# Turning both halves of a probability tile with one DMA in the first column group

## The chip, the cores and the metric

The kernel runs on one core of one Trainium2 chip. The core has a tensor engine (TensorE, PE, with its weight loads shown apart as PEld), a vector engine (VectorE, DVE), a scalar engine (ScalarE, ACT), a general engine (GpSimd, POOL), a queue engine (SyncE, SP) that issues DMAs, and 16 DMA engines. The metric is the device time of one execution in microseconds (us), less is better. Before the change it is 911.15 us, the median of three runs (909.12 to 911.76).

## The reference

The forward pass mixes two branches by a gate: `out = g * a + (1 - g) * b`, with `g = sigmoid(x . gate_w)`. Branch `a` is attention with 32 heads of 16 columns over 2048 rows, where row `q` sees the keys `q-255 ... q`; branch `b` is a gated feed-forward with 1376 hidden columns. The reference returns the output and, by automatic differentiation, the gradients of `x`, of the attention weights `wqkv` and `wo`, of the three feed-forward weights and of `gate_w`:

```
qkv = (x @ wqkv)                      # 32 heads of 16
scores = q k^T * 16**-0.5, masked to 0 <= q - k < 256
p = softmax(scores);  a = (p v) @ wo
b = ((relu(x Wg)) * (x Wu)) @ Wd
out, vjp = jax.vjp(f, x, wqkv, wo, Wg, Wu, Wd, gate_w);  grads = vjp(grad_out)
```

For the change only this matters: attention's backward pass needs the exponentials of the scores, P, and their products with the gradient scores, P*D, in both orientations. With keys on partitions they serve the sums over keys (output and gradient of q); turned, with queries on partitions, they serve the sums over queries (gradients of k and v).

## The kernel before

The program has three stages. The first (to about 258 us of the profiled span) does the feed-forward's forward and backward passes and writes three of its tensors to HBM. The second (258 to about 720 us) does attention, forward and backward, in four column groups `c` of 128 columns, that is 8 heads each. The third (to the end) forms the output and the gradient of `x` row block by row block.

The second stage is a list of turns (L633 to L661), 46 to a column group. A turn has two units (`x` = 0 and 1), each for two heads. A unit has one or two blocks of 128 queries by 128 keys. `pair_of(q)` is the diagonal block and the one below it for key block `q`; `edges_of` are the blocks at the window's far edge, two of them in one turn. For every two key blocks there are six turns, two of which are edge turns; every column group ends with four turns, the last with one block per unit.

In each turn the loop at L925 writes instructions in this order, by hand, and each engine runs its own in that order:
- `products` (L676): PE forms the scores S of this turn's two units and the gradient scores D of the turn before.
- `front` (L694): one exponential on ACT (L700) for both units, from S in PSUM to the tile `two` (called PP in the profile), 2 units x 2 kinds x 4 x 128 columns. Edge turns take the tile from another set, PPm. PP has 4 buffers and PPm 2.
- `mask` (L702): POOL zeroes what the window leaves out (L710).
- `gradp` (L714): one multiply on DVE (L717) writes P*D of the turn before, of both units, into the second half of the same tile.
- `flip` (L760) for units that are turned by DMA: one turn after their scores, on SP's queue.
- `some_sums`/`rowsum` (L726): PE multiplies P and P*D with K and V into the tile BA, at most five blocks a turn.
- `cd_piece` (L483): PE multiplies the turned tiles with the query rows into the tile CD (L492, L495), three turns or more after the query block is closed, in the order of key blocks.
- `flip` for the units that PE turns (L771): two turns after their scores, eight 128 x 128 transposes to PSUM, and a copy out (`share`, L80, which picks ACT or DVE by a running estimate; the copy is at L72 or L74).
- one or two pieces of background work: projections of the next rows and, from the second column group on, weight gradients.

So in the middle of the stage the unit `x` = 0 of every turn with two blocks is turned by a DMA of 8 blocks of 128 x 128 (256 KB), and the unit `x` = 1 by PE. Turns of the first two key blocks of the first column group, and of the last two of the last, are turned by PE alone. In the first column group there is no weight gradient yet in the background.

`place` (L743) gives a unit the tile of its turned blocks. For edge turns that is half of one of four `wide` tiles, taken once per turn; for others a tile of its own out of 14 (2 x 4 x 128 columns, 2 KB per partition each). The dictionary `P2` tells `cd_piece` where each block lies.

SP issues DMAs in the order written. In the stage these are the flips, the turned rows of Q and of the output's gradient (`rows`, L172, one per four row blocks), stores of finished rows (L506, 512 KB each), and loads of weights that the third stage needs (L523, turned on the way).

Of the kernel before, what the change touches and what calls it, by code (L numbers as in the profile page):

```python
# [11 lines left out]
BF = mybir.dt.bfloat16  # L12
# [10 lines left out]
def kernel(  # L23
# [20 lines left out]
    nc = tc.nc  # L44
    P = 128
# [9 lines left out]
    NT = S // P  # L55
    DC = D // P
# [23 lines left out]
    def share(out, in_, n, half=False, by=None, sbuf=False):  # L80
        cost = {"act": 0.11 + n * (0.00098 if sbuf else 0.00078),
                "dve": 0.08 + n * (0.00036 if sbuf else 0.00051 if half else 0.001)}
        eng = min(("act", "dve"), key=lambda e: busy[e] + cost[e])
        busy[eng] += cost[eng]
        if by is None:
            evac(out, in_, eng)
        elif eng == "act":
            nc.scalar.mul(out, in_, by)
        else:
            nc.vector.tensor_scalar(out, in_, by, None, op0=ALU.mult)  # L90
# [30 lines left out]
    def wide(name):  # L121
        return wq.tile([P, 2, 2, 4, P], BF, tag="m", bufs=4, name=name)
# [344 lines left out]
    if True:  # L467
# [4 lines left out]
        wk = p3b.enter_context(tc.tile_pool(name="attw", bufs=2))  # L472
# [3 lines left out]
        P2 = {}  # L476
# [157 lines left out]
        for c in range(DC):  # L634
            def pair_of(q):
                return [(q, q), (q + 1, q)]

            def edges_of(r):
                return [(k, k - 2) for k in (r, r + 1) if 2 <= k < NT]

            for q in range(0, NT, 2):
                if q + 2 < NT:
                    its = ((pair_of(q), 0), (pair_of(q), 2), (edges_of(q + 1), 0), (pair_of(q + 1), 2), (pair_of(q + 1), 0),
                           (edges_of(q + 2), 2))
                else:
                    its = ((pair_of(q), 0), (pair_of(q), 2), ([(q + 1, q + 1), (q + 1, q - 1)], 0), ([(q + 1, q + 1)], 2))
                for k, (blocks, g) in enumerate(its):
                    two = []
                    for x in range(2):
                        u = Unit()  # L650
                        u.c, u.q, u.g, u.x, u.blocks, u.nb, u.at = c, q + k // 3, g + x, x, blocks, len(blocks), len(turns_)
                        u.edge = blocks[-1][1] == blocks[-1][0] - 2
                        u.dma = x == 0 and len(blocks) == 2 and (c > 0 or q > 0) and (c < DC - 1 or q < NT - 2)
                        u.turn = u.at + (1 if u.dma else 2)
                        two.append(u)
                    turns_.append(two)
# [84 lines left out]
                BAsb[(u.c, qb)] = BAs  # L741

        def place(u):  # L743
            if u.edge:
                if u.at not in wides:
                    wides[u.at] = wide("p2")
                p2 = wides[u.at][:, u.x if u.nb == 2 else 0, :, :, :]
            elif u.nb == 2 or u.x == 0:
                p2 = wk.tile([P, 2, 4, P], BF, tag="P2", bufs=14, name="p2")[:]
                wides[u.at] = p2  # L750
            else:
                p2 = wides[u.at]
            for i, (qb, kb) in enumerate(u.blocks):
                b = 2 * (i if u.nb == 2 else u.x)
                P2[(u.c, qb, kb, u.g)] = p2[:, :, b:b + 2, :]
            return p2

        wides = {}

        def flip(u):  # L760
            p2 = place(u)
            if u.dma:
                nc.sync.dma_start_transpose(out=p2.rearrange("p a b q -> p (a b) q"),
                                            in_=u.PP.rearrange("p a b q -> p (a b) q"))
                return
            if u.nb == 2 or u.x == 0:
                pools["pt"] = ps.tile([P, 2, 4, P], BF, tag="tr", bufs=2, name="pt")
            pt = pools["pt"]
            for a in range(2):
                for b in range(2 * u.nb):  # L770
                    nc.tensor.transpose(pt[:, a, b if u.nb == 2 else 2 * u.x + b, :], u.PP[:, a, b, :], ident[:])  # L771
            return (lambda: share(p2, pt[:], 8 * P, True)) if u.nb == 2 or u.x == 1 else None
# [102 lines left out]
        with tc.manual_schedule():  # L875
# [49 lines left out]
            while turn < NI + 3 or ev or cdq or bg or sums:  # L925
# [9 lines left out]
                if us and (turn == 0 or turns_[turn - 1][0].q != us[0].q):  # L935
                    c, j = us[0].c, us[0].q
# [32 lines left out]
                for v in vs:  # L969
                    if v.dma:  # L970
                        flip(v)
# [10 lines left out]
                for w in flips.get(turn, []):  # L982
                    if not w.dma:
                        for f in copies:
                            f()
                        copies = [f for f in [flip(w)] if f]
# [165 lines left out]
```

## Time and profile before

| | |
|---|---|
| median of three runs | 911.15 us |
| the profiled execution's own time | 905.92 us |
| its span on the core | 904.2 us |
| mean granted TensorE clock | 0.992 |
| PE busy | 865.2 us, 96% |
| DVE, POOL, ACT busy | 492.8, 474.5, 389.9 us |
| transposes on PE (L771) | 1536, 117.9 us busy |
| copies of turned tiles on DVE (L74) | 167, 684 ns each |
| DMAs that turn tiles (L763) | 168, 4.4 us from issue to landing (median) |
| SP's DMA queue q1 | 133.13 MB, 81.7% of 16 engines' time |

Busy time of an engine is the time that its instructions cover; PE's matmuls overlap each other, so one of them may be listed with 220 ns and come 50 to 60 ns after the last. The share of a DMA queue is the time that its packets took, as a part of 16 engines' time; a packet that waits for its turn counts too, so a share near 100% does not say by itself that bytes move at the highest rate. "To landing" is the time from an issue to the last byte's arrival.

The first column group's turns lie between 258.04 us (its first exponential) and 360.96 us (the first of the second group).

### The profile page before, as it was taken

To read this page: it belongs to the slowest core of one execution; us is meant where nothing else is said; L and a number is where in the kernel's file an instruction comes from. 1 tells how busy PE (TensorE), PEld (TensorE's weight loads), DVE (VectorE), ACT (ScalarE), POOL (GpSimd) and SP (SyncE) were. 2 spreads that over 40 slices of the span, in tenths; PEclk is the share of its full clock that TensorE was granted. 3 is DMA by queue.
4 is the path that set the end of the run, shared out by engine and by line. 5 is a ranking of instruction groups with operands and counts; after the bars stand their busy time and mean duration, and the time that the engine had idled before them with its cause. 6 is when DMAs were issued, how large, how long until landed. Compare 5 with 4: busy or idle time off the path is not lost. (4 is left out here: it accounts for less than half of the span.)

```text
span 904.2 us, 29627 instructions
## 1 busy us (share of the span) xinstructions
PE 865.2 (96%) x12569; PEld 563.4 (62%) x12569; DVE 492.8 (55%) x754; ACT 389.9 (43%) x565; POOL 474.5 (52%) x883
## 2 busy tenths in 40 slices
PE   7999999999988999999999999999899999999998
PEld 4566555565657777777777767777577744444443
DVE  4543322233247888878778777788677322322322
ACT  5522222223247676666557655667464311111111
POOL 2544444454327777976668766687566512222221
PEclk9999999999989999999999999999899999999999
DMA  9989899988726999999978999999999996777750
GB/s 282 210 182 228 214 209 201 225 202 199 191 56 96 149 148 170 146 152 217 181 113 140 132 238 161 135 164 173 219 178 216 248 278 155 187 196 193 195 124 27
DMA packets 444334, 161.25 MB, mean 178 GB/s; under 512 B 362696, under 2 KB 441896, under 8 KB 444200
## 3 DMA queue, kind: packets, MB, share of 16 engines
q1 hardware_dynamic: 418520, 133.13, 81.7%
q10 hardware_dynamic: 23856, 20.98, 8.2%
q0 software_dynamic: 1824, 5.25, 1.7%
q8 instruction: 98, 1.61, 0.7%
q14 instruction: 36, 0.29, 0.1%
HBM read 38.44 MB, written 38.41 MB: 85 GB/s over the span
## 5 line engine op out<-in xcount | busy, mean ns | idle before, releaser
L717 DVE TENSOR_TENSOR PP<-PP,D 128x1024 bf16<-128x1024 bf16 (+1 forms) x184 | 219.5, 1193 | 69.4 <-POOL PP L710 24.9
L700 ACT ACTIVATE PP<-S 128x1024 bf16<-128x1024 f32 (+1 forms) x184 | 185.2, 1006 | 96.3 <-PE D L667 48.2
L710 POOL TENSOR_SCALAR_AFFINE_SELECT PP<-PP 128x512 bf16<-128x512 bf16 (+1 forms) x188 | 143.5, 764 | 108.8 <-ACT PP L700 93.4
L74 DVE COPY p<-pt 128x1024 bf16<-128x1024 bf16 x167 | 114.3, 684 | 16.5 <-PE pt L771 16.3
L771 PE MATMUL pt<-ident,PP 128*128 128x128 bf16 x1536 | 117.9, 221 | 1.7 <-DVE p L74 0.9
L350 POOL TENSOR_TENSOR hT<-rg,upm 128x512 bf16<-128x512 bf16 x44 | 52.4, 1192 | 126.1 <-DVE upm L348 105.4
L734 PE MATMUL BA<-KV,PP 128*128 128x33 bf16 x1440 | 106.6, 180 | 6.1 <-ACT BAs L72 6.1
L383 PE MATMUL wps<-dgu_r,x_r 128*128 128x256 bf16 x704 | 105.6, 272 | 3.7 <-DVE wst L74 3.4
L734 PEld LDWEIGHTS <-PP 128*128 128x128 bf16 x1440 | 85.6, 96 | 31.2 <-issue 11.2
L736 PE MATMUL BA<-KV,PP 128*128 128x17 bf16 x1440 | 102.2, 170 | 0.3 <-issue 0.3
L492 PE MATMUL CD<-rq,p 128*128 128x32 bf16 x1440 | 95.0, 176 | 0.0
L495 PE MATMUL CD<-rq,p 128*128 128x16 bf16 x1440 | 93.8, 169 | 1.1 <-issue 1.1
L736 PEld LDWEIGHTS <-PP 128*128 128x128 bf16 x1440 | 84.7, 96 | 13.5 <-issue 8.6
L383 PEld LDWEIGHTS <-x_r 128*128 128x128 bf16 x704 | 68.8, 98 | 35.7 <-issue 5.4
L771 PEld LDWEIGHTS <-PP 128*128 128x128 bf16 x1536 | 89.5, 98 | 2.0 <-issue 2.0
L667 PE MATMUL S<-zT,K 32*128 32x128 bf16 (+3 forms) x1056 | 78.4, 241 | 5.4 <-ACT PP L700 2.7
L495 PEld LDWEIGHTS <-p 128*128 128x128 bf16 x1440 | 80.6, 96 | 1.5 <-issue 1.2
L492 PEld LDWEIGHTS <-p 128*128 128x128 bf16 x1440 | 80.8, 96 | 0.3
L667 PE MATMUL D<-zT,V 32*128 32x128 bf16 (+3 forms) x1056 | 73.3, 239 | 4.1 <-DVE PP L717 3.6
L1072 ACT COPY a_sb<-aps 128x512 f32<-128x512 f32 x16 | 9.4, 586 | 145.9 <-issue 133.0
L348 DVE SCALAR_TENSOR_TENSOR upm<-rg,ups 128x512 bf16<-128x512 bf16 x44 | 30.2, 686 | 68.5 <-PE ups L336 43.8
L385 PE MATMUL dps<-db_r,h_r 128*128 128x512 bf16 x176 | 66.7, 379 | 0.0
(144 smaller groups left out, 1471.4 us busy)
## 6 DMA issues: line engine op xcount, KB each, us to landing
dqkvo_d<-rows_st SPq DMA_DIRECT2D x14, 512.0 KB, 4.7
hT_d<-hT ACTq DMA_DIRECT2D x44, 128.0 KB, 2.5
dgT_d<-dgu ACTq DMA_DIRECT2D x44, 128.0 KB, 2.9
duT_d<-dgu ACTq DMA_DIRECT2D x44, 128.0 KB, 2.8
duT_g<-duT_d SPq DMA_DIRECT2D x8, 640.0 KB, 5.3
dgT_g<-dgT_d SPq DMA_DIRECT2D x7, 640.0 KB, 8.0
gt<-hT_d SPq DMA_DIRECT2D x7, 640.0 KB, 5.8
dar<-da_d SPq DMA_DIRECT2D x16, 256.0 KB, 4.6
```

What stands on the lines that cost most here:

```text
L74: nc.vector.tensor_copy(out, in_)
L383: nc.tensor.matmul(acc["w"][:, c, :], lhsT=x_r[:, t, c * P:(c + 1) * P], rhs=k.dgu_r[:, :, i, :], start=(go_ and c % 2 == 0), stop=no_, sk ...
L385: nc.tensor.matmul(acc["d"][:], lhsT=k.h_r[:, i, :], rhs=db_r[:, t, :], start=go_, stop=no_)
L492: nc.tensor.matmul(cd[0][:, h, :], lhsT=p2[:, 0, pr, :], rhs=rq[:, h, 0:2 * Dh], start=cd[1], stop=True, skip_group_check=True)
L495: nc.tensor.matmul(cd[0][:, h, 0:Dh], lhsT=p2[:, 1, pr, :], rhs=rq[:, h, 2 * Dh:3 * Dh], start=False, stop=True, skip_group_check=True)
L667: nc.tensor.matmul(dst, lhsT=proj[(u.c, kb // TPG)][nm + ("", "1")[par]][rows[par], (kb % TPG) * P:(kb % TPG + 1) * P], rhs=proj[(u.c, qb ...
L700: nc.scalar.activation(two[:].rearrange("p x a b q -> p x a (b q)")[:, :, 0, 0:n], flat(us[0].S[:], n), ACT.Exp)
L710: nc.gpsimd.affine_select(out=out, in_=out, compare_op=ALU.is_ge, fill=0.0, base=0 if up else -1, pattern=[[0, 2], [0, b1 - b0], [1 if up ...
L717: nc.vector.tensor_tensor(out=v(1), in0=v(0), in1=flat(vs[0].D[:], n), op=ALU.mult)
L734: nc.tensor.matmul(BA[:, h, 0:33], lhsT=u.PP[:, 0, 2 * i + pr, :], rhs=kv[:, kb % TPG, h, 1:34], start=(first and pr == 0), stop=True, ski ...
L736: nc.tensor.matmul(BA[:, h, 33:50], lhsT=u.PP[:, 1, 2 * i + pr, :], rhs=kv[:, kb % TPG, h, 0:17], start=False, stop=True, skip_group_check ...
L771: nc.tensor.transpose(pt[:, a, b if u.nb == 2 else 2 * u.x + b, :], u.PP[:, a, b, :], ident[:])
```

## The change

In the first column group, from the third key block on, a turn with two blocks per unit has both units turned by one DMA of 16 blocks (512 KB). It is issued when the second unit's turn to flip comes, which for both is one turn after the scores. These units are turned on PE no longer, so their transposes and the copies out of PSUM are gone: 39 turns, 312 transposes, 39 copies. The number of SP's DMAs stays at 39 there.

For all column groups, the turned tiles of a turn that is not an edge turn lie in one tile of double size, 7 of them in place of 14 single ones. The bytes are the same. In the other column groups the first unit is still turned by DMA and the second by PE.

```diff
                         u.edge = blocks[-1][1] == blocks[-1][0] - 2
-                        u.dma = x == 0 and len(blocks) == 2 and (c > 0 or q > 0) and (c < DC - 1 or q < NT - 2)
+                        u.joint = c == 0 and q > 0 and len(blocks) == 2
+                        u.dma = (x == 0 or u.joint) and len(blocks) == 2 and (c > 0 or q > 0) and (c < DC - 1 or q < NT - 2)
                         u.turn = u.at + (1 if u.dma else 2)
...
         def place(u):
-            if u.edge:
-                if u.at not in wides:
-                    wides[u.at] = wide("p2")
-                p2 = wides[u.at][:, u.x if u.nb == 2 else 0, :, :, :]
-            elif u.nb == 2 or u.x == 0:
-                p2 = wk.tile([P, 2, 4, P], BF, tag="P2", bufs=14, name="p2")[:]
-                wides[u.at] = p2
-            else:
-                p2 = wides[u.at]
+            if u.at not in wides:
+                wides[u.at] = wide("p2") if u.edge else wk.tile([P, 2, 2, 4, P], BF, tag="P2", bufs=7, name="p2")
+            p2 = wides[u.at][:, u.x if u.nb == 2 else 0, :, :, :]
...
         def flip(u):
             p2 = place(u)
+            if u.joint:
+                if u.x == 1:
+                    nc.sync.dma_start_transpose(out=wides[u.at][:].rearrange("p x a b q -> p (x a b) q"),
+                                                in_=u.two[:].rearrange("p x a b q -> p (x a b q)"))
+                return
             if u.dma:
                 nc.sync.dma_start_transpose(out=p2.rearrange("p a b q -> p (a b) q"),
                                             in_=u.PP.rearrange("p a b q -> p (a b) q"))
```

## The prediction

> **What bounds the kernel now.** I read the page first (busy shares, then the DMA line), then the attention stage by its first column group alone: its groups of lines, its DMA traffic, and windows of one to two microseconds in it. The change touches only that group. Its exponentials (L700) count the turns: the first turn starts at 258.04 us, turn 6, the first that has a joint DMA, at 272.27, and the next column group starts at 360.96.
>
> The page's parts 1 and 3:
>
> ```profile
> PE 865.2 (96%) x12569; PEld 563.4 (62%) x12569; DVE 492.8 (55%) x754; ACT 389.9 (43%) x565; POOL 474.5 (52%) x883
> ...
> q8 instruction: 98, 1.61, 0.7%
> ```
>
> TensorE (PE) is busy everywhere, so 39 x 8 transposes less on it look like time won. Keep queue q8 in mind: 98 packets for 2 x 12569 PE and PEld instructions, one per 256 of them. These are fetches of PE's program.
>
> The DMA view of 277 to 359 us (the stage of the change; GB/s in 40 slices, packets, queues, issues):
>
> ```profile
> GB/s 52 79 128 73 189 191 138 160 165 131 128 71 168 95 113 153 114 277 194 88 268 109 192 136 128 136 128 128 72 226 238 70 194 270 96 264 96 226 146 166
> DMA packets 45179, 12.30 MB, mean 150 GB/s; under 512 B 44135, under 2 KB 45159, under 8 KB 45159
> q1 hardware_dynamic: 45159, 12.01, 100.8%
> q8 instruction: 15, 0.25, 1.2%
> dqkvo_d<-rows_st SPq DMA_DIRECT2D x2, 512.0 KB, 4.6
> p<-PP SPq DMA_TRANSPOSE x38, 4.2
> rows<-zT SPq DMA_TRANSPOSE x3, 4.9
> p<-in_A_wqkv_dram SPq DMA_TRANSPOSE x2, 3.9
> ```
>
> SP's queue already shows a share of 100.8% at 150 GB/s, while the slices swing between 70 and 277. A share near 100% can be time in which packets wait, so the next view asks what the queue can do. It is the windows view (PE, PEld, DVE, ACT and POOL busy; PE clock; DMA share; GB/s):
>
> ```profile
> 277.00:359.00 82.00, 79.11 (x1973) 62.32 (x1970) 72.12 (x103) 58.98 (x76) 64.95 (x146) 1.00 1.02 150
> 340.90:357.30 16.40, 16.18 (x405) 12.45 (x404) 14.33 (x21) 11.02 (x16) 12.85 (x31) 1.00 1.26 165
> 740.80:743.80 3.00, 3.00 (x16) 1.37 (x14) 0.40 (x1) 0.11 (x1) 0.58 (x1) 1.00 1.27 290
> 317.90:319.30 1.40, 1.09 (x32) 0.89 (x30) 1.25 (x2) 0.91 (x2) 0.78 (x1) 1.00 1.26 281
> 316.50:317.90 1.40, 1.40 (x36) 0.96 (x35) 1.26 (x2) 0.96 (x2) 1.35 (x4) 1.00 0.18 6
> 278.50:279.80 1.30, 1.30 (x28) 0.78 (x19) 1.30 (x2) 1.10 (x2) 0.79 (x4) 1.00 1.06 199
> ```
>
> Three rates of the same transposing traffic are to be seen. With a full queue it runs at 281 to 290 GB/s (740.8 is the 32-block transpose of L872). With an empty queue it runs at 199. And for 1.4 us, from 316.5, it stands at 6: in the packet records a q8 fetch of 16 KB starts at 316.02 and holds one of the 16 engines for 1.09 us, and the other engines' transposing packets stop until that engine has caught up. The packets of the stage show such a stop of 1.3 to 1.6 us beside almost every fetch. Where SP issues transposes without a pause (340.9 to 357.3, three fetches), 165 GB/s is what comes out.
>
> **The change part by part.** The turn now: 39 turns from 272.27 to 358.94, 2.22 us each.
>
> *PE transposes.* 39 units of 8 leave PE. One unit, from the timeline:
>
> ```profile
> 296.31 0.46 PEld L771 LDWEIGHTS <-PP 128*128 128x128 bf16 x8
> ```
>
> 39 x 0.45 us = 17.6 us of PE, all on PE's own path: 79.11 of 82 us are busy. This is the most that the change can win. POOL with 64.95 of the 82 us bounds it at about the same place (17 us).
>
> *Copies.* 39 copies of the transposed tiles leave: 33 of DVE at 684 ns (L74) and 6 of ACT at 1012 ns (L72). That is 22.6 and 6.1 us beside PE's work. DVE has 72.12 of 82 us in this stage, so this makes room and sets no end.
>
> *The wait of the DMA.* The joint DMA needs both halves of the tile PP. One multiply (L717) writes both, so it waits for nothing that the old DMA did not wait for, and it stands at the same place in SP's queue. The second half is now turned a turn earlier. Its first reader on PE (L492) comes 6 to 10 turns after its scores, in the order of the built program.
>
> *The tile of a turn.* 7 tiles of double size in place of 14: both halves of a turn are read by the same steps of L492, so the rotation frees them at the same turns as before. Nothing.
>
> *DMA work.* This is the price. 39 DMAs move 512 KB in place of 256 KB. 38 more x 262 KB are 10 MB on top of the 12.30: 22.3 MB where the queue has moved 12.3. Per turn, as S:
> - 524 KB at the rate of a full queue, 290 GB/s: 1.81 us.
> - Fetches: 15 now, 13 after, since 39 x 16 PE and PEld instructions less are 624 / 256 = 2.4 of them. 13 x 1.4 us / 39 turns = 0.47 us.
> - What else shares the queue: 3 + 2 transposes of 262 KB and 2 stores of 524 KB, 2.36 MB at 290 GB/s, 8.1 us, 0.21 us per turn.
> Sum 2.49 us, more than the turn's 2.22.
>
> The lower end is S = 2.02, no stop at all: a fetch that hits an engine while the others work on. The upper end is the rate of 340.9 to 357.3, 165 GB/s with its stops inside: 3.18 + 0.37 = 3.55. I take 2.60, near the sum, because a queue that is behind is a full one, and full queues show 281 to 290; the tenth is for stretches in which it runs dry. SP's time to issue 16 blocks is in no row: 8 blocks take 1.23 us at least, 32 take 5.9 and more (L872), while SP waits for room. Within S that lies between 1.3 and 2.9 us, and only the upper end would bind.
>
> The Trainium skill (Advanced Engine Details and Errata, X-Bar Transpose) says that transposing DMAs are as fast as plain ones and expects 350 to 400 GB/s. At 350 the 22.3 MB would take 64 us and would hide in the 82. This trace speaks against it: no window of transposes is above 290, and the stage's mean is 150 at a full share.
>
> *How late DMAs become time.* The tiles PP have 4 buffers for two turns in three and PPm 2 for the third, so the exponential of a turn waits until the DMA of the turn six before has read its tile. Now a DMA lands 4.4 us after issue (median) and nothing waits. With S above the turn, the queue falls behind until this wait binds, and then ACT, POOL, DVE and PE all go at S. The first joint DMA is issued at 277.32 and lands 4.4 + 0.9 us later, at 282.6. The DMA of turn 43 lands 37 x S later. It frees the tile of turn 49, whose exponential now starts at 367.02. The loss is 282.6 + 37 S - 367.02 = 37 S - 84.4 us: none at S = 2.28, 7.7 at 2.49, 11.8 at 2.60. After that the next column group turns 8 blocks by DMA per 2.46 us and the queue catches up; it is full of PE's work, so nothing is given back.
>
> PE's clock: it would idle some 25% of the stage. In 270 to 275 us it was busy 3.33 of 5 us and kept its full clock, so I count nothing; the half clock from 259.2 to 266.0 came after longer gaps and would cost some 3 us each time.
>
> Against the profiled execution: 905.92 + 11.8 = 917.7 us. Its span is 904.2, and the 1.7 around it stay. The median of the runs shown is 911.15, 5.2 above that execution, and the change is added to it: 911.15 + 11.8 = 923.
>
> **Rivals.**
> A, the faster side: fetches do not stop the joint transposes. For it: some fetches in the stage fall where the queue was empty and cost nothing. Against it: the six GB/s at 316.5 and the slices of 70 to 96. Then S = 2.02, 37 S - 84.4 = -9.7 us, 901. It decides from S below 2.28, where the stops cost less than 0.26 us per turn. The skill's rate above ends on this side too: then PE's 17 us would be all won, 894.
>
> B, the queue is fed no faster than an empty one runs: 199 GB/s (278.5 to 279.8), because SP issues late and each DMA starts from nothing. Then (524 + 60) KB / 199 = 2.93 us, plus a third of the stops that the feed doesn't cover, 3.1: +30 us, 941. For it: 165 GB/s in the stretch without pauses, where SP's issues follow each other at 1.4 us. Against it: 281 after each stop, in this same stage.
>
> C, nothing to be measured: S between 2.21 and 2.35. A change of 0.3% (2.7 us) is about what a measurement can tell from none.
>
> **How the numbers follow.** The forecast, S from 2.35 to 2.85: 0.50. B and beyond: 0.18. A: 0.20, of which 0.03 for the skill's rate. C: 0.12. So slower 0.68, same 0.12, faster 0.20. The time is that of S = 2.60, 923. The forecast's own range is 914 to 932. The 8 in 10 leave out a tenth of A's side and about a tenth of B's: 903 to 942.
>
> **What would show it.** In the profile after: the stage from 272 to 361 us longer, its GB/s near 220 and no slices of 70 to 130 but those of the fetches; DMAs p<-PP of the stage that land 9 to 13 us after issue; SP's issue of them over 2 us; ACT's exponentials waiting for "DMA p<-PP"; PE busy about 70% there. The page's chain would have to gain nothing after 740 us. Right in the sum, wrong in S: landings of 5 us and turns near 2 us. Wrong altogether: landings that stay below 6 us with turns still above 2.2, so that something other than the DMA holds the turn, or a half PE clock in the stage.

## The result and the profile after

The changed kernel takes 942.41 us, the median of four runs (939.37 to 945.54), against 911.39 us for the kernel before (four runs, 909.12 to 911.76). The ratio is 1.0348, with a 95% interval of 1.0315 to 1.0381: 31 us slower. The forecast was slower by 11.8 us, 923 us, its own range was 914 to 932, and its eight in ten ended at 942.

The profiled execution took 942.83 us, with a span of 941.1 us. Parts 1 and 2 of its page:

```profile
PE 856.1 (91%) x12130; PEld 553.9 (59%) x12257; DVE 475.0 (50%) x720; ACT 384.5 (41%) x560; POOL 474.7 (50%) x883
...
PEclk8999999999997655689999998999999999999999
...
GB/s 274 199 178 216 206 210 212 221 202 199 172 18 185 201 186 204 188 174 179 191 160 108 162 179 162 167 150 157 209 187 210 221 272 234 176 171 177 202 140 29
```

PE is busy for 9 us less, and yet the span is 37 us longer. TensorE's clock is low for long in one place, slices 13 to 18 (282 to 424 us), which is the first column group from its first joint DMA on, and the start of the second. By the first exponential of each column group, the first group takes 129.7 us (262.19 to 391.93) where it took 102.9, and the second 118.4 where it took 114.1. Together that is 31 us. Another 4 us of this execution lie ahead of attention, in work that the change does not touch, and 2 us in the third column group; after that both kernels take 314 us to the end.

The windows view of the stage (PE, PEld, DVE, ACT and POOL busy; PE clock; DMA share; GB/s):

```profile
281.00:391.00 110.00, 76.17 (x1699) 51.74 (x1713) 57.09 (x74) 54.83 (x72) 67.54 (x151) 0.65 1.18 192
```

No engine is busy for 70% of it. The DMA view of the same window, and what the line of the joint DMA says (its durations on SP in ns, who waited for it, issue to landing), with the line of the 8-block DMAs in the kernel before ahead of it:

```profile
q1 hardware_dynamic: 79557, 20.82, 117.2%
q8 instruction: 13, 0.21, 0.7%
```

```profile
L763 SPq DMA_TRANSPOSE p<-PP x168: 1231/1297/4285, 277.3 to 703.1; - x168
...
L759 SPq DMA_TRANSPOSE p<-PP x39: 1397/2591/4376, 281.1 to 399.2; - x39
...
  ACT PP L701: 41.4, 17
...
DMA to landing us min/median/max: 4.4/5.4/7.2
```

ACT's exponentials wait 17 times, 41.4 us in all, for a joint DMA; in the kernel before, nothing waited for one of the DMAs that turn tiles (L763). SP is occupied by one joint DMA for 2.6 us (median), where the 8-block ones took 1.3. The stretch from the timeline of SP, and that of ACT:

```profile
332.96 19.52 SPq L759 DMA_TRANSPOSE p<-PP  x7
```

```profile
346.93 1.02 ACT L701 ACTIVATE PP<-S 128x1024 bf16<-128x1024 f32 x1 [1.33 <-DMA p<-PP]
348.65 1.02 ACT L701 ACTIVATE PP<-S 128x1024 bf16<-128x1024 f32 x1 [0.70 <-PE D L668]
...
353.11 1.02 ACT L701 ACTIVATE PP<-S 128x1024 bf16<-128x1024 f32 x1 [2.26 <-DMA p<-PP]
...
398.56 1.02 ACT L701 ACTIVATE PP<-S 128x1024 bf16<-128x1024 f32 x1 [5.61 <-DMA p<-PP]
...
402.50 1.02 ACT L701 ACTIVATE PP<-S 128x1024 bf16<-128x1024 f32 x1 [1.09 <-PE S L668]
```

In this stretch SP issues one joint DMA behind the other without a pause, one per 2.8 us. Turn by turn the records show the wait of six turns: the multiply of turn 24 ended at 325.10, its DMA was issued at 336.12, when SP was through with those ahead of it; it landed at 340.58, and the exponential of turn 30, which writes the same tile, started at 340.69. Of the 29 exponentials of turns 18 to 46, 23 start within 0.15 us of the landing six turns back. The joint DMAs land 3.12 us apart on the mean (285.62 to 404.22, 38 intervals).

### The profile page after: what moved, and what is told of

Read it like the earlier page. It is cut to its first block, busy times and chain, and to the rows that moved or that the text cites. A ratio compares the mean times of both kernels' runs of the same rounds, so it can differ in the third digit from the quotient of the medians.

```text
span 941.1 us, 28831 instructions
## 1 busy us (share of the span) xinstructions
PE 856.1 (91%) x12130; PEld 553.9 (59%) x12257; DVE 475.0 (50%) x720; ACT 384.5 (41%) x560; POOL 474.7 (50%) x883
## 5 line engine op out<-in xcount | busy, mean ns | idle before, releaser
L711 POOL TENSOR_SCALAR_AFFINE_SELECT PP<-PP 128x512 bf16<-128x512 bf16 (+1 forms) x188 | 143.3, 763 | 142.2 <-ACT PP L701 127.0
L735 PEld LDWEIGHTS <-PP 128*128 128x128 bf16 x1440 | 87.7, 98 | 36.8 <-issue 18.9
L668 PE MATMUL S<-zT,K 32*128 32x128 bf16 (+3 forms) x1056 | 83.1, 256 | 26.0 <-ACT PP L701 21.8
L737 PEld LDWEIGHTS <-PP 128*128 128x128 bf16 x1440 | 86.3, 98 | 31.1 <-issue 27.9
L74 DVE COPY p<-pt 128x1024 bf16<-128x1024 bf16 x134 | 91.8, 685 | 15.5 <-PE pt L771 15.2
L771 PE MATMUL pt<-ident,PP 128*128 128x128 bf16 x1224 | 94.8, 223 | 1.0 <-DVE p L74 0.9
L495 PEld LDWEIGHTS <-p 128*128 128x128 bf16 x1440 | 81.6, 97 | 1.8 <-issue 1.5
L668 PE MATMUL D<-zT,V 32*128 32x128 bf16 (+3 forms) x1056 | 79.2, 255 | 3.5 <-DVE PP L718 2.7
L492 PEld LDWEIGHTS <-p 128*128 128x128 bf16 x1440 | 81.9, 97 | 0.3
L668 PEld LDWEIGHTS <-K 16*128 16x128 bf16 (+1 forms) x1056 | 36.7, 97 | 68.5 <-issue 61.9
L771 PEld LDWEIGHTS <-PP 128*128 128x128 bf16 x1224 | 72.3, 99 | 1.2 <-issue 1.2
```

The source lines that it names most:

```text
L74: nc.vector.tensor_copy(out, in_)
L492: nc.tensor.matmul(cd[0][:, h, :], lhsT=p2[:, 0, pr, :], rhs=rq[:, h, 0:2 * Dh], start=cd[1], stop=True, skip_group_check=True)
L495: nc.tensor.matmul(cd[0][:, h, 0:Dh], lhsT=p2[:, 1, pr, :], rhs=rq[:, h, 2 * Dh:3 * Dh], start=False, stop=True, skip_group_check=True)
L668: nc.tensor.matmul(dst, lhsT=proj[(u.c, kb // TPG)][nm + ("", "1")[par]][rows[par], (kb % TPG) * P:(kb % TPG + 1) * P], rhs=proj[(u.c, qb ...
L711: nc.gpsimd.affine_select(out=out, in_=out, compare_op=ALU.is_ge, fill=0.0, base=0 if up else -1, pattern=[[0, 2], [0, b1 - b0], [1 if up ...
L735: nc.tensor.matmul(BA[:, h, 0:33], lhsT=u.PP[:, 0, 2 * i + pr, :], rhs=kv[:, kb % TPG, h, 1:34], start=(first and pr == 0), stop=True, ski ...
```

## The experiments

One theory was tried against four rivals. The theory: SP's DMA queue needs more time for a turn's bytes than the turn had, and the loss is 37 S - 84.4 us, with S the queue's time per turn. The rivals: the form of one DMA with 16 blocks; the tile of double size; PE's half clock; a turn that would not have been faster with PE relieved. The chips differ, so each kernel has its ratio to the kernel before on the same chip, whose medians were 909.4 to 911.5 us.

**The tile alone.**

```diff
-                        u.joint = c == 0 and q > 0 and len(blocks) == 2
+                        u.joint = False
```

> Only the second part of the change: turned tiles of a turn in one tile of double size, 7 in place of 14; no joint DMA. Theory (DMA queue: the joint DMAs' bytes set the turn): as before, 911 within 3 us. Rival (the tile's rotation makes DMAs wait): some part of the 31 us, above 915.

Measured: 911.23 us, ratio 0.9995 [0.9971, 1.0019]. The tile of double size costs nothing that can be seen; the interval is -2.6 to +1.7 us.

**Two DMAs of 8 blocks in place of one of 16.**

```diff
             if u.joint:
-                if u.x == 1:
-                    nc.sync.dma_start_transpose(out=wides[u.at][:].rearrange("p x a b q -> p (x a b) q"),
-                                                in_=u.two[:].rearrange("p x a b q -> p (x a b q)"))
+                nc.sync.dma_start_transpose(out=p2.rearrange("p a b q -> p (a b) q"),
+                                            in_=u.PP.rearrange("p a b q -> p (a b) q"))
                 return
```

> Both units of a turn are turned by DMA, but each by its own DMA of 8 blocks, both issued one turn after the scores. Same bytes as the changed kernel. Theory (bytes in SP's queue set the turn): 937 to 948, turns of 3.0 to 3.2 us in the first column group. Rival (a DMA of 16 blocks is a slow form, its issue or its flow): below 925.

Measured: 949.74 us, ratio 1.0422 [1.0395, 1.0450], 7 us slower than the changed kernel and a little outside the range. The form of 16 blocks is not the trouble; for these bytes it is the better form. The last experiment comes back to this.

**PE's transposes kept.** The joint DMA stays, and PE turns the second unit as well, into PSUM, for nobody.

```diff
+                for w in (turns_[turn - 2] if 2 <= turn <= NI + 1 else []):
+                    if w.joint and w.x == 1:
+                        idle_turn(w)       # 8 transposes into a PSUM tile "tr"
```

> The changed kernel, and PE still does the eight transposes of the second unit into PSUM, two turns after the scores; nobody reads them and the copies stay out. PE has 17.6 us more to do and less time to idle. Theory (DMA queue): 939 to 946, with a granted clock nearer 1. Rival (PE's half clock, which the idle time brings, makes the loss): below 925.

Measured: 943.62 us, ratio 1.0343 [1.0312, 1.0373]. With PE's work put back the time is that of the changed kernel. The windows view of its stage:

```profile
281.00:390.00 109.00, 86.77 (x2003) 67.24 (x2003) 55.07 (x72) 52.23 (x70) 66.06 (x146) 0.86 1.18 191
```

The clock is 0.86 in place of 0.65, PE has 312 transposes more to do, and the queue moves its bytes at the same pace, 191 GB/s against 192. So PE's work is not in this time, and its clock, as far as 0.86 against 0.65 can tell, is not either.

**The second unit not turned.** The DMA of 8 blocks stays, and nothing turns the second unit.

```diff
-                if u.x == 1:
+                if u.x == 0:   # 8 blocks, of the first unit
...
-            p2 = wides[u.at][:, u.x if u.nb == 2 else 0, :, :, :]
+            p2 = wides[u.at][:, u.x if u.nb == 2 and not u.joint else 0, :, :, :]
```

> The first unit is turned by a DMA of 8 blocks as before the change, the second unit is not turned at all: its products read the first unit's turned blocks. Left out: the second unit's turned blocks in the first column group. It has the change's relief of PE, DVE and ACT without its DMA bytes. Theory (DMA queue): faster than before, 895 to 906, since PE's 17.6 us are partly won and the queue needs about 2.0 us per turn. Rival (a PE with less to do clocks down and the turn's chain of engines is the bound anyway): 908 or more.

Measured: 909.01 us, ratio 0.9972 [0.9957, 0.9987], 2.5 us faster than before. So even with its price left out, the relief of PE by 17.6 us, DVE by 22.6 and ACT by 6.1 brings 2.5 us. The theory's range, 895 to 906, was missed, and the rival's, 908 or more, was met. The windows show one thing that this rival names, a lower clock:

```profile
290.00:308.00 18.00, 15.85 (x416) 11.33 (x413) 12.52 (x18) 12.69 (x18) 15.09 (x34) 0.97 0.98 141
308.00:325.00 17.00, 16.32 (x342) 10.66 (x338) 10.13 (x13) 10.22 (x13) 12.53 (x28) 0.50 1.18 170
325.00:352.00 27.00, 24.23 (x621) 17.19 (x620) 19.75 (x27) 19.25 (x27) 23.50 (x53) 1.00 1.08 156
```

From 308 to 325 us TensorE had half its clock and did 342 matmuls in 17 us (20 per us); in the windows beside it, at 0.97 and 1.00, it did 23 per us. It had idled 12% of the first window; at half clock its records cover 96% of the second.

**The same, with a little work for PE.** Added to the last kernel: four transposes per turn that nobody reads, in place of the eight that the kernel before did.

```diff
+            for b in range(2 * u.nb):
+                nc.tensor.transpose(pt[:, 0, b, :], u.PP[:, 0, b, :], ident[:])
```

> The kernel in which the second unit is not turned (its products read the first unit's turned blocks; that part is left out), and PE does four transposes per turn whose result nobody reads, in place of the eight of before. It asks why that kernel won only 2.5 us of PE's 17.6: its clock fell to half for some 25 us of the stage. If the clock ate the gain: clock near 1 in the stage, turns of 2.0 to 2.1 us, 903 to 907. If the turn's chain of ACT, DVE and POOL is the bound anyway: 909 or more, turns near 2.2.

Measured: 904.61 us, ratio 0.9942 [0.9920, 0.9964], 5.3 us faster than before. By the two ratios, more work on PE made it 2.7 us faster; the interval of each ratio is 1.4 to 2 us to either side. The windows view of the same stretch:

```profile
308.00:325.00 17.00, 15.32 (x415) 12.27 (x418) 11.70 (x16) 11.31 (x15) 14.63 (x31) 1.00 1.15 178
```

Here the clock held. From 277 to 358 us it was 0.96 on the mean, where the kernel without the four transposes had 0.85 (277 to 357). The two profiled executions don't show the gain, though: 907.01 and 906.86 us, with turns of 2.17 us in both, where turns of 2.0 to 2.1 had been expected. Among the ten executions of this kernel time and clock go together: the six with a mean clock of 0.988 or more took 901.99 to 905.38 us, the four at 0.987 or less 906.58 to 909.61. That the clock took those 2.7 us is therefore likely and not shown.

In the Trainium skill, "TensorE: Matmul & The Clock Gate" (Part 1, What's actually happening) says that the gate passes half the clock after an idle window of about 3.4 us. Its two states are the ones seen here, 0.5 and 1.0, and the stretch of 17.07 us at half clock is five times its window of 3.41 us. The page speaks of idle windows; here the clock fell with PE's matmuls covering 88% of the window before (83% of its last 3.41 us), in many short waits.

**The dose.** The joint DMA in one turn in six, one in three, two in three; each kernel has one of the three new lines.

```diff
-                        u.joint = c == 0 and q > 0 and len(blocks) == 2
+                        u.joint = c == 0 and q > 0 and len(blocks) == 2 and k == 2          # 7 of 39 turns
+                        u.joint = c == 0 and q > 0 and len(blocks) == 2 and u.edge          # 13 of 39
+                        u.joint = c == 0 and q > 0 and len(blocks) == 2 and not u.edge      # 26 of 39
```

> The joint DMA in one turn in six of the first column group (the first edge turn of each six and the edge turn at the end, 7 joint DMAs). Theory (queue), 16 blocks in 2.5 us and 0.6 us of stops and other DMAs: 9.4 blocks on the mean, S = 1.46 + 0.6 = 2.06 us, below the turn's 2.22 and the 2.28 from which a loss begins. PE is relieved of 7 x 0.45 = 3.2 us, of which some 60% were won where nothing else was in the way: 908 to 911, against a kernel before at 910 to 911.5. Rival (any joint DMA hurts): above 912.

> The joint DMA in the edge turns alone, one turn in three (13 joint DMAs of 16 blocks; the other 26 turns as before the change). Theory (queue), with the changed kernel's own figures, 16 blocks in 2.5 us, 0.37 us of fetch stops and 0.25 us of other DMAs per turn: 10.7 blocks on the mean, S = 1.67 + 0.62 = 2.29 us, and the loss 37 S - 84.4 = 0.3 us: 909 to 915. Rival (each joint DMA costs in proportion, by a wait of its own): a third of 31 us, 921.

> The joint DMA in all but the edge turns, two turns in three (26 joint DMAs). Theory (queue): 13.3 blocks on the mean, S = 2.08 + 0.62 = 2.70 us, loss 37 x 2.70 - 84.4 = 15.5 us: 923 to 931. Rival (in proportion): two thirds of 31 us, 932.

| joint turns | S by the theory, us | loss by 37 S - 84.4, us | measured, us | ratio (95%) |
|---|---|---|---|---|
| 7 | 2.06 | none | 909.04 | 1.0003 [0.9982, 1.0025] |
| 13 | 2.29 | 0.3 | 912.39 | 1.0035 [1.0011, 1.0059] |
| 26 | 2.70 | 15.5 | 925.24 | 1.0161 [1.0128, 1.0193] |
| 39 | 3.12 (measured) | 31.0 | 942.41 | 1.0348 [1.0315, 1.0381] |

The loss is not in proportion: by the medians, the first 13 joint DMAs cost 2.4 us, the next 13 another 12.9, the last 13 another 15.7. So there is a threshold, between 7 and 26 joint turns, and the theory has it near 13. None of these kernels is faster than the one before. The seven joint DMAs were expected to win about 2 us by PE's relief; nothing of it is to be seen, and the interval ends at -1.6 us. That 15.5 and the 15.3 us of the medians agree so closely at 26 is partly luck: in the profiled execution the DMAs landed 2.78 us apart (turns 6 to 43) and not 2.70, the formula makes 18.5 us of that, and its first two column groups took 19.4 us longer than those of the profiled execution before.

**The rate by itself.** A program without the computation: transposes of 16 blocks from SBUF to SBUF on SP's queue, in stretches, each beside one kind of the attention stage's work. It was executed once.

```diff
+    for other in (None, lambda: dve(26), lambda: pl(40), lambda: act(30), lambda: pe(560), all4):
+        tc.strict_bb_all_engine_barrier()
+        turn16(12)
+        if other is not None:
+            other()
+    tc.strict_bb_all_engine_barrier()
+    turn8(24)
```

> Not the reference's computation: a program that only measures the disputed rate, with all outputs zero. Seven stretches, each of 12 transposes of 16 blocks from SBUF to SBUF on SP's queue (the last of 24 of 8 blocks): alone, beside DVE multiplies as L717's, beside POOL selects as L710's, beside ACT exponentials as L700's, beside PE matmuls with weight loads as L734's, beside all four, and last the 8-block ones alone. If 2.5 us per 16 blocks (210 GB/s) is the queue's own pace for transposes within SBUF, all stretches show 200 to 215 GB/s. If it comes from the engines' traffic in the attention stage, the first shows 280 to 290 (1.81 us) and one of the others falls to 210.

The windows view, in the order of the stretches (alone; DVE; POOL; ACT; PE; the stretch meant for all four; 8 blocks alone), then PE's stretch before its first fetch, and that fetch. In the sixth stretch ACT's work came only after its DMAs, from 207.7 us on, so DVE, POOL and PE are beside them there:

```profile
12.00:40.00 28.00, 0.00 (x0) 0.00 (x0) 0.00 (x0) 0.00 (x0) 0.00 (x0) 1.00 1.13 210
44.00:72.00 28.00, 0.00 (x0) 0.00 (x0) 27.25 (x23) 0.00 (x0) 0.00 (x0) 1.00 1.13 210
77.00:105.00 28.00, 0.00 (x0) 0.00 (x0) 0.00 (x0) 0.00 (x0) 22.85 (x36) 1.00 1.14 211
109.00:137.00 28.00, 0.00 (x0) 0.00 (x0) 0.00 (x0) 27.14 (x28) 0.00 (x0) 1.00 1.13 210
142.00:173.00 31.00, 12.58 (x464) 12.25 (x461) 0.00 (x0) 0.00 (x0) 0.00 (x0) 0.70 1.15 187
178.00:206.00 28.00, 12.11 (x459) 11.68 (x455) 27.25 (x23) 0.00 (x0) 22.84 (x36) 0.80 1.22 195
242.00:272.00 30.00, 0.00 (x0) 0.00 (x0) 0.00 (x0) 0.00 (x0) 0.00 (x0) 0.50 1.01 191
140.50:143.30 2.80, 2.80 (x106) 2.80 (x103) 0.00 (x0) 0.00 (x0) 0.00 (x0) 1.00 1.16 206
143.40:145.00 1.60, 1.60 (x67) 1.60 (x64) 0.00 (x0) 0.00 (x0) 0.00 (x0) 1.00 1.25 30
```

Alone, with a full queue, 16 blocks run at 210 GB/s, 2.50 us. DVE, POOL and ACT, each by itself beside them, change nothing (210, 211, 210). Beside PE it is 187, and in that stretch lie four fetches of its program: at 143.4 the rate falls to 30 GB/s. From 140.5 to 143.3, where PE works and no fetch has come yet, it is 206 GB/s, so the loss comes with the fetches and not with PE's work. 187 GB/s over 31 us are 5.8 MB, which at 210 take 27.6, so the four fetches cost 3.4 us, 0.85 each. In the sixth stretch the same count gives 2.0 us for three to four fetches, 0.5 to 0.7 each; in the changed kernel's window, 20.82 MB in 110 us, it leaves 10.9 us for 13 fetches, 0.84 each. They cost less than they last because the queue catches up after each: in the records some 1120 packets per us for about 2 us, 287 GB/s, where it otherwise moves 835. The stretch with 8 blocks runs at 191 GB/s with one issue per 1.375 us, 2.75 us for 16 blocks: 0.25 more per turn, 10 us over 39 turns, where two DMAs in place of one had cost 7. SP is occupied for 1.33 us by each of these issues and they land 3.2 to 3.5 us after it, so nothing piles up behind them: this pace may be SP's own and not the queue's, which was not tried.

## Why the prediction was wrong

The step that failed is a term of the sum: "524 KB at the rate of a full queue, 290 GB/s: 1.81 us". It is 2.50 us. The two windows that carried it were something else. The one at 317.9 us is a queue that catches up after a fetch, which in the changed kernel's records lasts 1.1 to 2.9 us and no longer. The one at 740.8 us is a transpose whose source lies in HBM; in the records it too follows half a microsecond of near standstill, so which of the two made it fast is not known. The third window, 199 GB/s, was read as a queue that starts from nothing; it was near the pace itself. With the measured figures the sum comes near: 2.50 for 16 blocks, 14 fetches x 0.85 / 39 = 0.31, and 2.36 MB of other DMAs, by an estimate at 210 GB/s too, 11.2 us / 39 = 0.29, give S = 3.10; with 0.5 us a fetch it is 2.97. Measured: 3.12. The forecast's S was 2.60.

What the other steps made of it, one by one:
- The loss as a function of S was right: 37 x 3.12 - 84.4 = 31.0 us, and 31.0 us were measured. As S is taken from the same run, this tests the formula alone, and the agreement to the tenth is luck. The last wait for a joint DMA is that of turn 47, at 398.56, whose tile turn 42's DMA frees; turn 49, from which the formula was made, started at 402.50 after a wait for PE, 2.5 us after its tile came free. From turn 47, which started at 363.38 before, the formula would be 282.6 + 36 S - 363.38, 31.5 us at 3.12. The threshold of 2.28 us agrees with the dose.
- Rival B had the price, S = 3.1 and 941 us, and a chance of 0.18. Its mechanism was half right: not, with 16 blocks, that SP issues late, but that the pace of transposes within SBUF is near 200 GB/s whether the queue is full or not.
- Fetches were put at 1.4 us each, as long as the rate was seen to stand still. They cost 0.5 to 0.85, since the catching up afterwards was not counted. This error and the first came from the same windows: the burst was taken for the rate, and so the stop for the whole price of a fetch.
- The wait of six turns was right, and its place not quite. The DMAs were to land 9 to 13 us after issue; they land 5.4 us after it, and the waiting is before the issue, on SP (11 us after the multiply in the case of turn 24). Two signs of "wrong altogether" came with this: landings below 6 us with turns of 2.90, and half a clock. Neither meant what it was named for: the DMA does hold the turn, from SP's side, and with PE's transposes kept the time is the same at 0.86 of the clock.
- "17.6 us of PE, the most that the change can win" was far from what any run won: 2.5 us without the second unit's turning, 5.3 with four transposes of it left. What held those turns at 2.17 us was not tried. Rival A's -9.7 us was for a queue without stops, and no run came near it.
- PE's clock was counted at nothing, from 270 to 275 us where it was busy 3.33 of 5 us and kept it. It fell to 0.65. In the changed kernel that cost nothing that the kept transposes could win back; in the kernel without the second unit's turning it may have cost half of the gain, by the medians.
- SP's time to issue 16 blocks, bounded by 1.3 and 2.9 us, is 1.32 us on an empty queue in the rate program, and 1.4 to 4.4 in the kernel, where SP is held while the queue is behind. With 16 blocks it binds nothing of its own: 1.32 is far below 2.50.
- The tile of double size, the order on SP and the third stage came out as said. So did PE's share of the stage (69%; 70% was named) and the wait that showed it; the GB/s are 192, not 220.
- On the page's rule that was weighed: the Trainium skill (Advanced Engine Details and Errata, X-Bar Transpose) expects 350 to 400 GB/s. Transposes from SBUF to SBUF, alone on the core, were at 210.

## What to carry to other kernels

Work that leaves a busy engine for a DMA queue has to be priced at the queue's lasting rate in that very form (source, size, issuer), taken from a stretch of many DMAs; the windows of 1 to 3 us used here showed a burst or a stop, not a rate. Where tiles come round after n turns, a queue that is slower than the turn shows nothing at first and then sets the pace for all engines, so the loss has a threshold and is found from S x turns, not from the added work. And relief of the busiest engine can be worth far less than its busy time, here 2.5 to 5.3 us of 17.6; idle time that it brings can lower the clock, which is to be looked at in the same windows.

## What the runs showed of the hardware

A fetch of PE's program (16 KB, one per 256 of PE's instructions) nearly stops the transposes of all 16 engines, to 6 and 30 GB/s in windows of 1.4 and 1.6 us, and then they run at 287 GB/s for 1.1 to 2.9 us. What stops them all, while the fetch itself takes about 0.95 us, the runs don't show. Without fetches the pace is 210 GB/s at 16 blocks per DMA and 191 at 8, and the work of DVE, POOL and ACT, one at a time, does not change it (210, 211, 210). Why the queue is faster for about 2 us after a stop than in the long run was not tried and stays open; so does why transposes in the feed-forward stage, with SBUF as source too, show bursts of 113 packets per 0.1 us in the packet records.
